# A new order, engine assignment and buffer choice for the same work: pooled attention with a gated convolution feed-forward, one Trainium2 core

## The chip, the core and the metric

The kernel runs on one core of one Trainium2 chip. A core has the matrix engine (PE, whose weight loads are shown apart as PEld), the vector engine (DVE), the activation engine (ACT), the general engine (POOL) and a queue engine that issues transfers (SP). Each runs its own instructions strictly in the order in which the program lists them, and waits on semaphores for the others. The metric is device time in microseconds (us) of one execution; the median of three runs is 651.73 us, from 650.28 to 654.78.

## What is computed

Four batches, eight heads, 1152 keys, head size 64. Queries are averaged in pairs, so 576 queries per head. The attention output, 512 features wide, goes through a feed-forward layer with a three-tap convolution in its gate.

```python
q_pool = q.reshape(B, H, S // 2, 2, D).mean(axis=3)
scores = np.matmul(q_pool, k.transpose(0, 1, 3, 2)) / np.sqrt(D)
attn = softmax(scores);  x = attn @ v            # (4, 576, 512) over all heads
h = np.maximum(x @ w_in, 0.0)                    # (4, 576, 1024)
gate = sigmoid(conv3(h, conv_w))                 # three taps along the sequence
out = (h * gate) @ w_out                         # (4, 576, 512)
```

## The kernel before

The program builds a list of 2470 tasks, each with an engine, what it must come after and the buffers that it uses. `Plan.order` (line 62) does not search at run time: it reads three tables. `SWAPPED` names the tasks that run on their other permitted engine, `SLOTS` gives the buffer of each ring that a task takes, and `ORDER` lists the tasks in the order in which they are written out. That fixes the queue of every engine. The numbers given to `add` as costs are not used by `order`, so they leave no mark in the program.

Two heads make a pair; there are 16 pairs, and each has five blocks of 128 queries (the fifth holds 64 of both heads). A block of one head goes through this chain:

- `scores` (L436, PE) multiplies queries and keys into a PSUM tile `s`, of which there are two. `top` (L448, DVE) finds the row maximum, `expo` (L453, ACT) takes the exponential and the row sum into `p`. The `s` tile is free again when `expo` is done. There are 144 of each.
- `total` (L466 on ACT or L470 on DVE) and `inverse` (L476, DVE) make the reciprocal of the sum.
- For most heads `high` (L500 on ACT or L495 on POOL) writes the normalised row in half precision into `hl`, `low` (L503, DVE) writes the remainder, and a transposing transfer (L516, SP) brings both to `pt`. For seven heads `norm` (L534 ACT, L538 POOL or DVE) keeps full precision, PE transposes (L552) into a PSUM tile `a`, of which there are two as well, and ACT copies it out (L557).
- `values` (L582, L588, PE) multiplies by the values; L598 (ACT), L604 or L606 (ACT or POOL) and L611 (DVE) split the result `x` in two halves.

Per batch, `feed` runs over groups of tokens and eight slices of 128 hidden features: `mm` (L671, PE), `relu` (L677, ACT), `tap0` (L684 on ACT or L688 on POOL), two more taps (L695, DVE), `tanh` (L701, ACT), `gate` (L705, DVE). `second` (L873, L879, L885, PE) multiplies by `w_out`, and L899 (ACT) copies out. Queries arrive by a transfer and are first added in pairs by `sum_q` (L289, POOL or DVE), then scaled by ACT (L292, L296). The early part of the kernel also takes the weights apart (L962 to L999).

Of the kernel before, what the change touches and what calls it, by code (L numbers as in the profile page):

```python
# [99 lines left out]
jNeldwkgdxdyj6kuj4khkOdzbFkvbGkidAkPkqdDbhkRehj7emkrkGj5kwbHkxkSkyksbsdtkTbIkBkzkCkHkDkEdEbJk6kjkQkAbKk9kUkFkV  # L100
bLk7kWk3kkk4kZklenbtk0buk5k8bvkmkolabweolokpbMbxknlbeCkXlpbyk1k2lrdKd3dJbQbCbRkKlcbSdLldlsllbTlqbUlmkYlebVltbz
b5lffvlGlnkLbDlubAlJlveFlHlDlhdMlglKlwlidOb6ljdPlkb7lzlLlElxlylYb8lFlIdQb9dRlBcalMdScbmjlZdTeHlNdUl0mklOdXlCdY
mmlAl1cclVlTl2mnl3lPlUlQlRcdeJmbdNmllWbWeGbBmol6eId4l4mBd5lSmpd6l5mEmqmCmrbXmcl7lXmymFmwl8l9mad7mxbYmumDmzd8eW
mTbZmGmAd9b0eamsb1mHmvmImUmJnbmtb2ebmVb3mMecmOb4efmNmWmPnckImdcemQedmKmXmfepkMmLjdmRmYeendmZkJejm0mSegm8eYkNne
m9mgcfmhnOm1nfnaeqcgm2ngmem6chjeerntcinhm3nicjm7nPnqm4e0nGeZjhnuckm5njnrnvclnsjinknQnwcmnRnxminHnBnIn6cwnlnSny
eBe1nmnonnnJnTn7DanpnUnVDCnzDbnWDXnZnADDcxesnXDoDYDEcyDcDFn8n0DdooczDeDpDGn9cADHDqopDZn2n1DfnEn3nFD0n4cBDJn5D1
cCDIDrD2nCoaDKoqDhDLDsobcDorD3cEocnDoGodoscnDioeohfdnKnYofDtDjDkotDMDlDuDmouDnovoHowoknLozcoomoJoxnMonoloicpoI
oKffDQojoLoEcqogoYnNcrDRoMDgDSD4csoFoNoZoOfheEctoyfiDvcuD5oPoReupmcvDwo0evDxoUcFewexD6oAeyoVpjo1D7ezD8oBo2eAoW
oSpko6eDoXfPoToCo3pbDyetpnoQplo4oDD9cGDzo5poEao9cHpEcIpcDNppDAcJfgpBpqcKpafwpucLo7pCprpzo8pApvpxpwcMpyEbpFcNpD
pGDTpTcOpsfceVDOpWpHEcpUpteKEdpfeLpIpXpJpMeMEecPpKpVcQpYEffyqbpZDBp0DUp1pNp4qcqtpgpOp2Egp5Eip6quqdpLcRp7EjcSp8  # L110
p9EkeOqeePqvcTeQEleRpRf6qfqap3cUpPqOeSqgqwqxqBeTqRqhqiqPqmpQpSfzcVqpDVeUqnqqqoqrqSqjeXqGqQeNqkqyEmqsqlqzqTq2fA
cWfBDWEhqUqAq5qVDPqWq3qZEwfNqHqXe3ERExq0qYq4EKq6EyEnEzq7q1rgEAEoESq8rjq9rhrdrae4ELe5fQrkqCETqEqFriEpe6rbEMEUrc
rlrxENe7reEBruqDqKECEOrfe8EPrmrve9rnryrorrEqrprwrsrqrzrIfbrAsdqLrBErrJrFrCrtEYfSseEssfEDrDrZEQrKrErGEEr2rLr0EF
EZrMr3rHrNrOr4E0EVr1rPEGsgfar5rQEWr6rRsar7shr8EtsiE1EHr9sbEIEusjfRsrEJskEvE2EXscsosuE4ssE5rVsvstfeslspsmswsFrS
# [1076 lines left out]
```

## Time and profile before

| | |
|---|---|
| median of three runs | 651.73 us (650.28 to 654.78) |
| the profiled execution | 651.88 us, of which the span of the trace is 650.1 us |
| PE busy | 585.3 us, 90% of the span |
| DVE busy | 580.9 us, 89% |
| ACT busy | 514.1 us, 79% |
| POOL busy | 163.9 us, 25% |

An engine's busy time is the time in which one of its instructions was running. Idle time is put down to whatever ended it. Two engines are near 90%, so the question for any stretch of the kernel is which of the two has the fewer gaps there, and what ends these gaps.

### The profile page before, as it was taken

The page shows a single profiled execution, that of the slowest core. Times are in us where ns is not written, and L with a number is a line of the kernel's source. Part 1 is how long each engine was busy: PE and PEld are TensorE (multiplying, and loading weights), DVE is VectorE, ACT ScalarE, POOL GpSimd, SP SyncE. Part 2 cuts the span into 40 slices and gives each one's busy share as a digit, 9 for nine tenths or more (in the row PEclk, how much of TensorE's full clock was granted, in tenths as well). Part 3 has the DMA queues.
Part 4 walks back from the last instruction along what each step waited for, and adds up shares of the span by engine and source line. Part 5 has one row for each costly group of instructions (what it writes and reads, how often), then busy time and mean ns, then how long its engine had stood idle before and what let it go on. Part 6 is the DMA issues. An engine that isn't in the chain of part 4 may idle for free. (4 is left out here: it accounts for less than half of the span.)

```text
span 650.1 us, 11849 instructions
## 1 busy us (share of the span) xinstructions
PE 585.3 (90%) x4394; PEld 364.9 (56%) x4394; DVE 580.9 (89%) x930; ACT 514.1 (79%) x959; POOL 163.9 (25%) x174
## 2 busy tenths in 40 slices
PE   3578887889998899999999899999999879999997
...
GB/s 302 176 188 202 187 155 148 160 160 125 164 142 218 130 184 171 180 211 173 218 138 219 175 207 182 169 211 182 199 163 200 199 152 129 200 111 151 91 34 40
DMA packets 276569, 109.61 MB, mean 169 GB/s; under 512 B 264864, under 2 KB 265376, under 8 KB 276512
## 3 DMA queue, kind: packets, MB, share of 16 engines
...
q8 instruction: 34, 0.56, 0.4%
...
## 5 line engine op out<-in xcount | busy, mean ns | idle before, releaser
L453 ACT ACTIVATE p<-s,sm 128x1152 f32<-128x1152 f32 x144 | 175.1, 1217 | 65.6 <-DVE sm L448 33.1
L436 PE MATMUL s<-kt,qt 64*128 64x512 f32 (+3 forms) x704 | 190.1, 484 | 34.0 <-ACT p L453 24.8
L448 DVE TENSOR_REDUCE sm<-s 128x1 f32<-128x1152 f32 x144 | 193.0, 1347 | 7.4 <-PE s L436 6.7
L503 DVE SCALAR_TENSOR_TENSOR hl<-p,sm,hl 128x1152 f16<-128x1152 f32 (+1 forms) x116 | 172.5, 1493 | 13.8 <-POOL hl L495 9.1
L436 PEld LDWEIGHTS s<-kt,qt 64*128 64x128 f32 (+1 forms) x704 | 92.2, 178 | 137.6 <-issue 79.6
L436 PE MATMUL s<-kt,qd 64*128 64x512 f32 x256 | 149.2, 665 | 0.0
L495 POOL TENSOR_SCALAR hl<-p,sm 128x1152 f16<-128x1152 f32 (+1 forms) x54 | 73.2, 1356 | 208.0 <-DVE sm L476 135.8
L582 PE MATMUL a<-pt,v 128*64 128x256 f16 (+2 forms) x1566 | 119.5, 271 | 0.4 <-ACT h L677 0.4
L671 PE MATMUL a<-x,wi 128*128 128x257 f16 (+3 forms) x864 | 104.8, 274 | 3.1 <-ACT pt L557 1.0
L582 PEld LDWEIGHTS <-v 128*64 128x64 f16 x1566 | 92.1, 110 | 10.3 <-issue 3.9
L671 PEld LDWEIGHTS <-wi 128*128 128x128 f16 x864 | 77.1, 98 | 29.5 <-issue 9.9
L879 PE MATMUL a<-wo,g 128*128 128x512 f32 x192 | 89.3, 606 | 0.7 <-DVE vs L334 0.7
L500 ACT ACTIVATE hl<-p,sm 128x1152 f16<-128x1152 f32 (+1 forms) x62 | 77.3, 1250 | 7.0 <-DVE sm L476 6.6
L695 DVE SCALAR_TENSOR_TENSOR g<-h,cw,g 128x255 f32<-128x255 f32 (+3 forms) x144 | 67.5, 488 | 4.7 <-ACT g L684 3.0
L552 PE MATMUL a<-ident,p 128*128 128x128 f32 (+1 forms) x315 | 49.8, 284 | 18.3 <-ACT pt L557 9.4
L588 PE MATMUL a<-pt,v 128*64 128x256 f32 (+1 forms) x252 | 64.3, 409 | 0.3 <-ACT pt L557 0.3
L879 PEld LDWEIGHTS a<-wo,g 128*128 128x128 f32 x192 | 34.6, 192 | 37.2 <-issue 34.9
L552 PEld LDWEIGHTS a<-ident,p 128*128 128x128 f32 (+1 forms) x315 | 33.3, 146 | 32.9 <-ACT pt L557 11.6
L557 ACT ACTIVATE pt<-a 128x384 f32<-128x384 f32 (+2 forms) x98 | 44.1, 473 | 8.1 <-PE a L552 7.8
L677 ACT ACTIVATE h<-a,bs 128x257 f32<-128x257 f32 (+3 forms) x72 | 33.8, 470 | 18.7 <-PE a L671 14.0
L688 POOL TENSOR_SCALAR g<-h,cw 128x255 f32<-128x255 f32 (+3 forms) x27 | 20.0, 743 | 102.2 <-ACT h L677 84.2
L538 POOL TENSOR_SCALAR p<-p,sm 128x1152 f32<-128x1152 f32 (+1 forms) x16 | 23.5, 1466 | 77.6 <-DVE sm L476 63.4
...
## 6 DMA issues: line engine op xcount, KB each, us to landing
...
```

The costliest lines, as they stand in the source:

```text
L436: nc.tensor.matmul(out=w, lhsT=f, rhs=kk, start=True, stop=True)
L448: nc.vector.tensor_reduce(out=sm[:, e:e + 1], in_=runs(st[e]), axis=AX.XY, op=ALU.max, negate=True)
L453: nc.scalar.activation(out=p.tile().rearrange("p (a n) -> p a n", a=2), in_=runs(st[e]), func=AF.Exp, bias=sm[:, e:e + 1], scale=1.0, accu ...
L495: eng.tensor_scalar(out=hl[rows, 0], in0=ps_[e][rows], scalar1=sm[rows, 6 + e:7 + e], scalar2=1.0, op0=ALU.mult, op1=ALU.mult,)
L500: nc.scalar.activation(out=hl[rows, 0], in_=ps_[e][rows], func=AF.Copy, scale=sm[rows, 6 + e:7 + e])
L503: nc.vector.scalar_tensor_tensor(out=hl[rows, 1], in0=ps_[e][rows], scalar=sm[rows, 6 + e:7 + e], in1=hl[rows, 0], op0=ALU.mult, op1=ALU.s ...
L552: nc.tensor.transpose(w[:, (i - a1) * nq:(i - a1 + 1) * nq], ps_[e][rows, i * P:(i + 1) * P], ident[rows, rows])
L582: nc.tensor.matmul(out=to, lhsT=o.v[:, e, c, vc:vc + D], rhs=o.pt[y, e][:, hl * NC + c, 0:n], start=(c == 0 and j == 0), stop=(c == NC - 1 ...
L588: nc.tensor.matmul(out=to, lhsT=o.v[:, e, c].bitcast(F32), rhs=p32.rearrange("p (a n) -> p a n", a=NC)[:, c, 0:n], start=(c == 0), stop=(c ...
L671: nc.tensor.matmul(out=w[:, 0:n], lhsT=wi[:, a, j, f * P:(f + 1) * P], rhs=x.x[:, c, s0:s0 + n], start=(i == 0 and j == 0), stop=(i == 2 a ...
L695: nc.vector.scalar_tensor_tensor(out=c, in0=h[:, t:t + tok], scalar=cw[:, f, t:t + 1], in1=c, op0=ALU.mult, op1=ALU.add)
L879: nc.tensor.matmul(out=w.tile(), lhsT=g[f // 4][:, f % 4, c:c + P], rhs=wo[:, f, :], start=(f == 0), stop=(f == FC - 1),)
```

## The change

`ORDER` and `SLOTS` are new throughout and `SWAPPED` names 170 tasks where it named 193. 155 tasks have another engine. Counted by line the engines change as follows; all else stays on its engine.

| task | before | after |
|---|---|---|
| `tap0` | 45 ACT, 27 POOL | 61 ACT, 11 POOL |
| `high` of the scores | 62 ACT, 54 POOL | 65 ACT, 51 POOL |
| `high` of x | 22 ACT, 14 POOL | 24 ACT, 12 POOL |
| `norm` | 16 POOL, 12 DVE, 7 ACT | 18 POOL, 10 DVE, 7 ACT |
| `total` | 48 ACT, 32 DVE | 45 ACT, 35 DVE |
| `sum_q` | 9 POOL, 7 DVE | 8 POOL, 8 DVE |
| last join of the weights (L999) | 6 POOL, 11 DVE | 4 POOL, 13 DVE |
| first half of v (L368, L373) | 10 ACT, 6 POOL | 9 ACT, 7 POOL |
| first half of w_out (L809, L813) | 4 ACT | 3 ACT, 1 POOL |

Two cost numbers in `add` are new as well. The diff, with one line of each table:

```diff
 ORDER = """
-cYaacXc1c2aucZc0abbNc3acadc4aehOafagahavaihRajhPaEdhawdihQhSh6axhTayazhUbOhVhWh9aAh7aFh3aBhXaGh8iaaChZioh4c5aD
...
+cYaacXc1c3bNauabcZc2acadc4aehOafagahbOaihRajhPavaEc0awhQdihSdBdhh6bPhTaxayhUhVazhWh9aAh7h3aBh1c6h4h8hZiaaCaFio
...
 SWAPPED = """
-aiaMaWa6bqbwbybVcdcmcvcEcWc1dfdldFezeTeYfyfJf4gkgBgJgUhbhhhJhUiciuiwiDiMi1i3i6jhjpjrjyjJjQjZkhkqkwkykBkMlelllu
...
+aiaMaWa6bqbwbybMbVb4cdcmcvcEcWc1dfdldFedeTe9fyfJf9gBgJgUg0hbhhhJhUiliuiwiDiMi3i6jpjJjQkjkqkykBkMkUlclelllMl1mp
...
         o.qts = [tq] + [
-            add("ACT", act(K1, 0.03), lambda e=e: turn_q(e), after=[t], uses=[o.qin] + ([o.qd] if e else []),
+            add("ACT", act(K1, 0.16), lambda e=e: turn_q(e), after=[t], uses=[o.qin] + ([o.qd] if e else []),
...
-            t = add("ACT", act(tok, 0.14), tap0, alt=("POOL", 0.28 + tok / 1400.0, True), after=[t] + cw_ready, uses=[h] + ([] if first else [g]),
+            t = add("ACT", act(tok, 0.14), tap0, alt=("POOL", 0.36 + tok / 1500.0, True), after=[t] + cw_ready, uses=[h] + ([] if first else [g]),
```

Three places show what this does to the queues. The first is DVE in batch 2, where the profiled execution stood at 355 to 363 us. `p` is the exponential of a block, `hl` its normalised halves, `sm` its sums. Before:

```order
L376 SCALAR_TENSOR_TENSOR v<-vin,vs,v 128x9x64
L538 TENSOR_SCALAR p<-p,sm 128x1152
L476 RECIPROCAL sm<-sm 128x2
L503 SCALAR_TENSOR_TENSOR hl<-p,sm,hl 128x1152
L448 TENSOR_REDUCE sm<-s 128x1
```

The same place on DVE in the change:

```order
L470 SCALAR_TENSOR_TENSOR sm<-sm,small 128x2
L476 RECIPROCAL sm<-sm 128x2
L705 SCALAR_TENSOR_TENSOR g<-g,h 128x255
L326 TENSOR_SCALAR vs<-vs 128x1
L503 SCALAR_TENSOR_TENSOR hl<-p,sm,hl 128x1152
L334 TENSOR_REDUCE vs<-a 128x1
```

Between the reciprocal and the L503 that needs the row normalised with it there was nothing, and now there are two short instructions. The `high` between them moved from POOL (L495, followed there by a `sum_q`, L289) to ACT (L500), and that `sum_q` moved to DVE, further on.

The second place is DVE one batch earlier, at 281 to 288 us of the profiled execution, with the names of before. Before:

```order
L476 RECIPROCAL sm<-sm 128x2
L503 SCALAR_TENSOR_TENSOR hl<-p,sm,hl 128x1152 x2
L470 SCALAR_TENSOR_TENSOR sm<-sm,small 128x2
L476 RECIPROCAL sm<-sm 128x2
L448 TENSOR_REDUCE sm<-s 128x1
L503 SCALAR_TENSOR_TENSOR hl<-p,sm,hl 128x1152
```

In the change:

```order
L448 TENSOR_REDUCE sm<-s 128x1
L503 SCALAR_TENSOR_TENSOR hl<-p,sm,hl 128x1152
L448 TENSOR_REDUCE sm<-s 128x1
L476 RECIPROCAL sm<-sm 128x2
L503 SCALAR_TENSOR_TENSOR hl<-p,sm,hl 128x1152
L448 TENSOR_REDUCE sm<-s 128x1
```

Here it is the other way round: a maximum (L448) stood between the last reciprocal and the last L503, and now it stands ahead of the reciprocal, with `high` still on POOL.

The third place is a `tap0` of batch 1 that POOL ran at 248 us, between two `high`. POOL before:

```order
L289 TENSOR_TENSOR qin<-qin 128x640
L368 TENSOR_SCALAR v<-vin,vs 128x18x64
L495 TENSOR_SCALAR hl<-p,sm 128x1152
L688 TENSOR_SCALAR g<-h,cw 128x321
L495 TENSOR_SCALAR hl<-p,sm 128x1152
```

ACT in the change, where the same `tap0` now stands (`h` is the hidden slice, `g` its gate, `cw` the taps):

```order
L598 ACTIVATE xf<-a,vs 128x256
L453 ACTIVATE p,sm<-s,sm 128x1152
L677 ACTIVATE h<-a,bs 128x323
L684 ACTIVATE g<-h,cw 128x321
L677 ACTIVATE h<-a,bs 128x323
L453 ACTIVATE p,sm<-s,sm 128x1152
```

The `tap0` moved from a queue that is idle three quarters of the time to one between two exponentials, right behind the `relu` (L677) that makes its input.

## Rows read from the trace of the kernel before

**Rows 1.** Stretches: us, busy us (instructions) of PE, PEld, DVE, ACT, POOL; clock, DMA, GB/s.
```profile
0.00:50.00 50.00, 27.64 (x109) 15.44 (x109) 41.26 (x66) 39.64 (x74) 10.70 (x15) 0.83 0.81 225
50.00:250.00 200.00, 177.73 (x1306) 115.99 (x1308) 191.85 (x307) 176.25 (x340) 65.75 (x64) 0.98 0.72 163
250.00:500.00 250.00, 241.88 (x1757) 146.76 (x1752) 230.66 (x342) 201.44 (x348) 58.49 (x62) 1.00 0.96 187
500.00:550.00 50.00, 43.22 (x348) 27.29 (x346) 47.80 (x73) 34.95 (x59) 11.22 (x12) 0.97 0.89 161
550.00:650.10 100.10, 94.80 (x882) 59.47 (x880) 69.34 (x146) 61.77 (x141) 17.73 (x22) 1.00 0.53 108
```

**Rows 2.** Chain that ended last, its end: start us, us, what.
```profile
622.45 0.87 issue
623.32 0.70 ACT o L899
...
633.31 9.06 PE a L873 x42
```

**Rows 3.** Groups by shape: line engine op, count | busy us, mean ns | idle before.
```profile
L448 DVE TENSOR_REDUCE sm<-s 128x1 f32<-128x1152 f32 x144 | 193.0, 1347 | 7.4 <-PE s L436 6.7
...
L453 ACT ACTIVATE p<-s,sm 128x1152 f32<-128x1152 f32 x144 | 175.1, 1217 | 65.6 <-DVE sm L448 33.1 <-DVE hl L503 16.5 <-POOL qin L289 2.8
...
L503 DVE SCALAR_TENSOR_TENSOR hl<-p,sm,hl 128x1152 f16<-128x1152 f32 x109 | 161.7, 1490 | 13.7 <-POOL hl L495 9.1 <-ACT hl L500 4.0
...
L500 ACT ACTIVATE hl<-p,sm 128x1152 f16<-128x1152 f32 x60 | 74.8, 1250 | 7.0 <-DVE sm L476 6.6
...
L557 ACT ACTIVATE pt<-a 128x384 f32<-128x384 f32 x84 | 38.6, 483 | 6.1 <-PE a L552 5.8
...
L684 ACT ACTIVATE g<-h,cw 128x255 f32<-128x255 f32 x20 | 10.0, 504 | 0.1
...
L684 ACT ACTIVATE g<-h,cw 128x321 f32<-128x321 f32 x15 | 8.4, 560 | 0.2
...
L538 DVE TENSOR_SCALAR p<-p,sm 128x1152 f32<-128x1152 f32 x7 | 6.7, 952 | 0.0
...
L289 DVE TENSOR_TENSOR qin<-qin 128x640 f32<-128x640 f32 x7 | 5.7, 814 | 4.2 <-DMA qin<-in_q_dram 4.2
...
L999 DVE TENSOR_TENSOR wo<-o,wo 128x512 f32<-128x512 f32 x6 | 4.1, 681 | 0.0
```

**Rows 4.** Line L503, the remainder on DVE: duration ns min/median/max.
```profile
L503 DVE SCALAR_TENSOR_TENSOR hl<-p,sm,hl x116: 1397/1410/2730, 19.7 to 600.0; 128x1152 f16<-128x1152 f32 x109, 64x1152 f16<-64x1152 f32 x7
```

**Rows 5.** Timeline at 357 to 363 us, DVE, then POOL: start us, us, instruction, [idle before].
```profile
357.71 0.17 DVE L476 RECIPROCAL sm<-sm 128x2 f32<-128x2 f32 x1 [0.22 <-ACT sm L466]
359.23 2.69 DVE L503 SCALAR_TENSOR_TENSOR hl<-p,sm,hl 128x1152 f16<-128x1152 f32 x1 [1.35 <-POOL hl L495]
...
357.97 1.23 POOL L495 TENSOR_SCALAR hl<-p,sm 128x1152 f16<-128x1152 f32 x1 [4.78 <-DVE sm L476]
359.16 1.54 POOL L289 TENSOR_TENSOR qin<-qin 128x640 f32<-128x640 f32 x1
```

**Rows 6.** Waits over the whole span: us in total, times, longest us.
```profile
ACT p L453 <- DVE sm L448: 33.1, 33, 3.4
...
PE s L436 <- ACT p L453: 24.8, 30, 2.4
...
DVE hl L503 <- POOL hl L495: 9.1, 9, 1.5
...
DVE sm L448 <- PE s L436: 6.7, 14, 1.0
...
DVE hl L503 <- ACT hl L500: 4.0, 6, 1.3
```

**Rows 7.** Timeline of the start, ACT, then PE.
```profile
7.81 1.28 ACT L296 ACTIVATE qd<-qin 64x512 f32<-64x512 f32 x2
...
8.97 1.19 PE L436 MATMUL s<-kt,qt 64*128 64x512 f32 x1 [8.97 <-DMA kt<-in_k_dram]
```

More of the change, by code (lines that the diff above doesn't have):

```diff
@@ L100 @@
[L100 to L114, printed above, removed]
@@ new lines @@
+h2aGc5ibdlaHaDiricaIdmakidaJdnhXipiedoilaKisdCh5h0iqifimhYalaLihiGc7amaMitanaoaNiJapaOdFaqiuardGiviHiiasigijdH
+c8iKiDatdaiIaYdbiEaPiYiwiLiFaQdcaRikddaSiMixdIiNaTaZdeiOiZizdWiyiniViBjja0a1i0iWiCaUa2iTiXdfjkjmiAiUaViPjli1iR
+a3dkjndZiQjEa4i2joa5c9i6iSjBdgd0a6jpd1i9aWi7jajCi3a7bijbaXjqi8i4a8jyjDi5jzd2djjTjFjrjAbjjcbkdpjGjujUjwa9jWjHei
+bljvdEbajxjIbmjJjsjXjQjfjVdJbnjRdqbobbjYbcbdjtjZj0bpj8kbbqdrj9kebebrjOdselkcjgbEjPjSdujKdvkdj1dwjMkfjLktdxjNbf
+kgdybgj4kuj6j5bFdzj2kOkvbGbHdAkhbIj7dDkRkwkikPemkakqbhkGj3bJdtkxkrenkjdVkBekkQkSkybskzkCkHkDkEbtkTk6buksbvkUkF
@@ new lines @@
+kkkVk7k3kWkok9kpk4eokAkmbKkllabwk8k1k5knbxlbkZlobQk2eCbRlcdKlrldbSk0lpllkXlekKbylsbAkYlmbTltbUbCbVbzb5lqljdYlG
+fvbDlndLlJkLlulvbLlkdMlwlHlDdOlhdPeFlilKlxb6lzlylAb7lflElBlLb8lIlFlYdQb9dRcalMmjlCdSlNlZlglOcbeHmkdTlRl0lTcclS
+mmcdlUlVdUbWlPbBdXl1mbeGehlQl2mllWl3mnl6bXl4dNd3mBmobMbYl5mpmEd4mqmCmymcd5lXl7mFmrl9l8mamDd6mzmsd8mtmTbZmGmAd9
+b0mweab1mHmumImUb2nbmJmvmxebmVb3epmKefmQmOeImWncmdkMkImPb4mLmMkJjhcemfecjdeWmXedmNjimYkNeemZjem0mRcfm8cgnemSm1
+mgm9m4mhndm6nfeYejm7ntnangchmem2cinOm3nhcjm5ninunqcknGe0egnPd7njeqnvnre1clnwnQnknxcmnRmiercwnBnsnHn6nIesnynSnl
@@ new lines @@
+nmeZnonJnnnznpDanTn7nADXcxDbcynUDcfdDCnVczDYnZnWcAn2DdDDcBDEn0nXooDZn3n1DFDon8nYD0opcCn4Dpn9cDn5oqDGeED1nCoaff
+nED2orDqnFobcEDhDecnDrnDeBocD3odDsoeDQosohDioGofetDjDtDfnKDHDkcoDgDlotcpcqDuDmcrouDRovoHowDScsoxctoknLoJolDToy
+oIozomoKoionoYnMojcuoLDnogDvcvoMfhoNoZoODJDwoRoPcFeupmf6DxDKDyo0DIoEevDzoSnNoFpjoTDUo1ewfgexeyoWfiezpkoUoXDLoV
+oCeAoAoDcGeDpboQplcHcIo2cJo3pno6oBfwcKpoDMo9o4pBcLpccMpapEDApCppcNo7D4pqo8pucOpDo5pFprpvD5pTpweJpseKpxeLpUptEb
+pGDBD6DNpWcPpHD7pypID8eVEcpzcQEdpXpJpfpMpKpVeMfypApLpYcRcSpZp0cTp1qbp4pgp2p5D9pNp6qcpOp3p7cUeOqtp8EeqdePpPqupR
@@ new lines @@
+DVpQqepSeQcVqvp9qfEiDOqaEfqgeReSqRcWeTqhqiDWqmDPqOeUqjqPEjeXqpfzqnqqqkqoqrEkqGfAElqlqwEgEmfBqxEhEnqSqyqQeNEofN
+qTqzq2qUqsqVq5qAqZqWq3EpqHqXEwq0q4qYEqq6fQrgErExq7ERq1EyrhqBe3rjEse2q8ESq9EzfcrardqErke4qFETqCe5reriEKEtrlrurb
+rfqDrxEUrvqKrmrce6EVEarne7roryrrrwrprsrzrIrqELEArZEWe8rArJEBqLEYrtrBEXrKr0rCrFEZrDrLEMe9rMECrEEDrGfSr1r2fbfaEE
+E0rNr3EFrHfTrOr4sdEGr5rPsgr6ENr7serRrQEusar8sfEOEHE1r9shfREIsbsisrE2EvscsuEJsjEPskssslsorVsvfUfesmswspstsnsIrS
+EQsFsxsyE4sCE5E6sGsqsDsHE7szsJf7sEsTfksAE8sKsUsBsLsMsVE9sNfjsOtaFaE3sQtdtbflfmtcfnFcsRf9FdfogaftfppdteFefqphsS
@@ new lines @@
+qItffstosWqJgbtgfrtrrWsXthfusYtptisPs2rTsZrXqMtjtqs0FfrUs1tss3tls4tCtks5ttperYFuqNtuFgtvtDtzFIFvtAtFgcFwgoFJFx
+FWtEtmFKFBtGtntwt4FLFXtHtxs6fxFMFytIpitJt5tNgqt6tQtOs7FztTFNtRtPFYtKGhgrFCs8FAFPFOGiFZtUFDfMfDtBFiFEFQFRFFs9tS
+fEFjFSt7tyF0FGt8tLGjt9FkFTgsFHGktMtVulfFfGuauotWGlumGaFbucfHuntXuptYFlfPFUfIGbtZfJF3FVuqfKuDfLurF4uGt1fOuEudgt
+ust2ubGmF5GcuHutFmt3uFGouuF1uwuIuYgHt0F2F6GpGduVfVuJGnuKueuOuBuWuzuvuCuLuAuxuZGJuyuXuMuRgGvdFhuSgnGeu0F7uTveuU
+uPgJvvvfuQvgGfu1fWu2u3GKFovhgKgLuhu4gMgYvwvivjvkGgvlvQfXu6u5uiFpvmF8vofZFqf0uNvxvRFrvyf1vzGQvDFsvAGqu9vBGRvavb
@@ new lines @@
+u7f2g0vTu8vSGrf3vrvUf4vcvsvCGLvtvpGsfChCfYv4vVf5F9f8GSvWv7v5vnvqvuvIvXv8v1vYGtv2vZv9GvGuvJv0GTgeGMGUvGv6GNwwGw
+v3wawbwiwcwxGxGCvHwdwfgXFtGVHbwjwyFnwgGDwlGOGEwkvEwmvFwKGywhwnGFgfGGwowzGPwpggwqwLvMweg1wtwAHcGHwuwrwMghwNGzwB
+w1GWwsgiGIHdwOgjG4wPgkw2GAHewvwCw4gmG5M6wQGXvNG6HfglHiGYG7gpGZwRG8HgG0HjwDw5wEwHw6wFHkwSG9wIw3wGxfw7w8Hhxiw9xg
+wTwJG1xhxaG2gvxjxcHlxbguHaxkxdxtHmG3wUxlGBxexwxmxuHpxnHogdgwHqg2gxxxxvHrxoxqgygzgAHsgEgBxrxyxHxpgCvKwVxKg3xIwX
+gDxJxzvLxsxAxLxBxExCychfxFxMxDHtwWxNufxOgFydxSujxVvOxGHuxTxPx4xWyevPxXughhyqx5x6hjx7yfxQhkHOwYyrxRIgHPygHQInIh
@@ new lines @@
+    "11032113002110221310211320100031303210100112102321100112031020023020101041310221001100213101022302032111012031"
+    "01002110101100210021113122012110130020312000213141102011230203112310110212231010003131231030000110020021101001"
+    "01220020110101203002132140302003011303021111011020131001132100200001110010003112111100311120300011101312200020"
+    "31001011110031030112123001311000020203032100301010011100000301031212102101103113002100211200131110211001130200"
+    "1131012321010110001100"
@@ L159 @@
+mymHmQmZm1nqnwnynBnMnUnZocouoMoOoRo1ppprpupJpMp4qjqmqwqyqUqWq8rdrrrCrLrNr5sjsosLsNs4titutKtYufujurutuwuLu1u3vo
+vyvDvOvWvYwowqwtwCwHwNwVwZw7xcxExYx0ynyPy0zbzlzzzLzZz4AdAoAwAEAMA0A5BgBjBsBDBFB1B6ChCkCyCMCSC8DLEyFDGqGxGLGSJc
+KhKvL8MUNe
 """
```

63 lines of the change are left out of this document (20 added, 43 removed).

## The prediction

> **What bounds the kernel now.** I read the busy times in five stretches first [rows 1]. The reader should look for the engine with the least idle time in each, because that one sets the pace. From 0 to 50 us the kernel fills: DVE is idle for 8.7 us, PE for 22.4. From 50 to 250 us DVE sets the pace, idle for 200 - 191.85 = 8.2 us, while PE is idle for 22.3 and ACT for 23.8. From 250 to 500 us PE does, idle for 8.1 us (DVE 19.3). From 500 to 550 us it is DVE again, idle for 2.2 us, and from 550 us on PE, idle for 5.3 us. PE's figure is the softer one, since its matmuls are pipelined. Added up, the engine that sets the pace is idle for 8.7 + 8.2 + 8.1 + 2.2 + 5.3 = 32.5 us; without the filling it is 23.8 us. That is all that a new order can win without taking work off PE and DVE. The chain that ended last shows at its end what little is left there: PE's products in a row, broken by a wait of 0.87 us and a copy of 0.70 us [rows 2].
>
> I then asked what ends the gaps. DVE waits 13.1 us in 15 places for a `high` before its L503, and 6.7 us in 14 places for scores; PE waits 24.8 us for exponentials, ACT 33.1 us for maxima [rows 6]. ACT and POOL are never the engine with the least idle time [rows 1].
>
> **The change, part by part.** The sum is made against the profiled execution: 651.9 us, of which 1.8 us lie around the span of 650.1. That is 0.2 us over the median of the runs.
>
> *Load.* No arithmetic is added, so PE's load is unchanged. DVE gets two joins at 0.68 us, one `sum_q` at 0.81 and three sums that I put at 0.15, a little under the 0.17 of a reciprocal of the same size [rows 5], and loses two `norm` at 0.95: 1.36 + 0.81 + 0.46 - 1.90 = **+0.7 us**, and I take it as on the path, since DVE sets the pace for 250 us. ACT gets 16 `tap0`, 11 of them of some 255 columns at 0.50 us, 3 of 321 at 0.56 and 2 short ones that I put at 0.3 (below both rows), with three `high` at 1.25 and two more halves of x, which I put at the 0.50 of the shorter `tap0`. It loses three sums, at DVE's 0.15, and one piece of v and one of w_out, for which I take 0.8 and 1.1, between the `tap0` and the `high` of twice the length. Together 5.5 + 1.7 + 0.6 + 3.8 + 1.0 - 0.5 - 1.9 = 10.2 us [rows 3]. ACT is idle for 650.1 - 514.1 = 136 us, 23.8 of it in the stretch from 50 to 250 us, so I cost it at nothing. If that cover fails it costs up to the whole 10.2 us; that is rival C. POOL loses 20 of its 168 instructions and is idle for three quarters of the span: nothing. The two new cost numbers leave no mark in the program.
>
> *Waits for `high`.* The reciprocal and the L503 that follows are both on DVE, with a `high` on another engine between them. What DVE does between the two is the cover. I went through both orders, gave each instruction its mean time from the trace, and took it as short wherever the cover is less than the other engine's instruction and 0.1 us. I did the same for the other waits of this kind on DVE (an exponential before a sum, a `tanh` before a gate, and so on). Before, 33 places are short by 14.1 us together; in the change 32 by 14.4. They are other places. At 359 us the cover was nothing, and DVE waited 1.35 us [rows 5]; with the gate now in between it would be short by 0.8. At 284 us a maximum of 1.35 us [rows 3] covered the `high`, and now nothing does, so 1.4 us is late there that was not. Stalls of over 1 us are six before and six after. The sum gets **+0.3 us**. Its ends are none of the 13.1 us that DVE now waits for `high` [rows 6], and twice that.
>
> *DVE and POOL in each other's way.* The L503 at 359.23 us took 2.69 us, where the median of all 116 is 1.41 [rows 4, 5]. It started when its `high` on POOL was done, and at that moment POOL began the `sum_q` behind it, which ran until 360.70; 360.70 - 359.23 = 1.47 us, and the 1.22 us left are a little less than a normal L503. The 109 L503 of the main shape together are 161.7 - 109 x 1.41 = 8.0 us over that median [rows 3]. The 20 instructions fewer on POOL are 12% of its count, so I take **-1.0 us**; the ends are 0, if other POOL instructions hit instead, and -8.0, if all such meetings go.
>
> The Trainium skill, page "SBUF — State Buffer", section "Who interferes with whom", has a rule for this: a DVE instruction with two inputs in SBUF and a GpSimd instruction that reads SBUF share a port pair, the first to start holds it throughout, and the other blocks entirely. The trace agrees: 2.69 us against 1.41. By that rule it is not the number of POOL instructions that counts but which of them stands ready behind a `high` whose L503 is waiting. I count five such places before and five in the change, so by the rule this term would be 0 and the sum 1.0 us higher.
>
> *PSUM tiles.* A block of scores can start when the exponential of the block two before has freed its `s` tile: a maximum of 1.35 us and an exponential of 1.22, with the steps around them 2.7 us [rows 3]. I added PE's instructions between one block and the next in the same tile. It is less than 2.7 us at 12 places before, short by 8.8 us together, and at 9 in the change, short by 6.5. For the `a` tiles I set 0.6 us, one copy of 0.48 [rows 3] and the steps around it: 48 places short by 11.4 us, and in the change 37 by 6.7. Most of that lies before 250 us, where PE's waits cost only what reaches DVE, that is some of the 6.7 us of waiting for scores [rows 6]. Scaled by 6.5 / 8.8 it is 1.7 us less. Between 250 and 500 us, where PE sets the pace, `s` gets 1.2 us worse and `a` 2.1 us better. Together **-2.6 us**; the ends are 0 and the whole 7.0 us.
>
> *Start and end.* At the start the two L296 and the L292 change places around the L962. The first score waits for its keys until 8.97 us, and the L296 end at 9.1 anyway [rows 7]; nothing. The last products, from 633 us on, stand in the same order [rows 2]: nothing.
>
> Sum: 651.9 + 0.7 + 0.3 - 1.0 - 2.6 = **649.3 us**.
>
> **The rivals.**
>
> *A, the forecast: waits change places and the sum of them stays.* For it: 33 short places against 32, loads within 1 us. Within 1% of 651.7, that is 645.2 to 658.2, about what a measurement of this kernel can tell from no change. Also here belongs the case that the new order lies in the slack altogether and nothing moves (652).
>
> *B, faster: the new order closes gaps that my local count doesn't see.* The pace-setter's 23.8 us are many short gaps, and only some of them are waits that a count of cover finds. PE's tiles do get more cover in the change. If four tenths of the 23.8 us go, the time is 651.9 - 9.5 = 642.4 us. Against it: the same number of stalls of over 1 us.
>
> *C, slower: ACT's queue.* ACT runs in order, and the 16 `tap0` now stand between exponentials. Where an exponential is already awaited, each delays it by 0.5 us, and with it the next scores, maxima and L503. Up to the 72nd exponential ACT has 6 us more ahead of it. It decides from the point at which ACT's idle time in 50 to 250 us, 23.8 us, is no longer where the exponentials need it. If all 10.2 us land on the path, with the +0.7 and +0.3 above and none of the gains, it is 663; with most of it, 660. Against it: ACT itself waits 33.1 us for maxima [rows 6], so it often is early.
>
> *D, slower: DVE blocked by POOL.* If behind each of the six stalls of over 1 us in the change a ready POOL instruction starts first, as at 359 us, that is 6 x 1.3 = 7.8 us; 649.3 + 1.0 + 7.8 = 658. Against it: before has the same pattern, and its cost is in the 651.9 already.
>
> **How the numbers follow.** A 0.51, B 0.31, C 0.11, D 0.07. The likeliest is A, so 649.3 us, with 645 to 654 as its own range. For 8 in 10 the range reaches from 639 us, at which over half of the 23.8 us would be gone, to 658.5, which takes in D: what stays out is the far end of B (0.1) and most of C (0.1). Faster by over 1% is B with 0.02 of A's lower end: 0.33. Slower by over 1% is C, half of D and 0.02 of A's upper end, rounded up: 0.17. The rest, 0.50, is within 1%.
>
> **What would show it.** In the profile of the change the table of stretches should have DVE idle for about 8 us and PE for about 8 us where each sets the pace; under 4 us in both is B. DVE's waits for `high` should again be about 13 us, with one of over 1 us at the second place shown above, and PE's wait for exponentials below 24.8 us. ACT's busy time should be about 524 us and POOL's about 149. If the group of L503 falls well under 1.49 us in the mean, the POOL term was too small; if DVE's waits for exponentials and sums grow by several us and ACT's wait for maxima shrinks, it is C. The prediction is wrong if short gaps, which a count by place can't see, add up to more than the four terms do.

## The result, and the profile after

| | before | change |
|---|---|---|
| first measurement, median | 651.38 us | 645.82 us (641.79 to 646.64) |
| ratio, 95% interval | | 0.9897 (0.9860 to 0.9933) |
| second measurement, median | 651.95 us | 646.02 us (644.50 to 646.61) |
| ratio, 95% interval | | 0.9882 (0.9848 to 0.9917) |

The change is faster by 5.6 to 5.9 us, on the border of the 1% that the forecast called no change. It lies in the range (639.0 to 658.5), 3.3 to 3.5 us under the forecast of 649.3, about halfway from there to the 642.4 us of rival B.

Two profiles of the change were taken. The first is the quickest of its twelve executions, 641.79 us; the second, from the repeat e9 below, is typical at 645.7 us. The busy times of the first, from its page, and of the second:

```profile
PE 579.7 (91%) x4394; PEld 362.0 (57%) x4394; DVE 577.5 (90%) x934; ACT 523.2 (82%) x975; POOL 155.2 (24%) x154
```

```profile
PE 582.3 (90%) x4394; PEld 363.3 (56%) x4394; DVE 580.0 (90%) x934; ACT 523.9 (81%) x975; POOL 153.8 (24%) x154
```

The stretches of the first profile, to lay beside [rows 1] (same columns), and those of the second:

```profile
50.00:250.00 200.00, 178.76 (x1322) 115.66 (x1321) 194.39 (x311) 182.15 (x351) 65.61 (x59) 1.00 0.77 166
250.00:500.00 250.00, 242.81 (x1817) 149.53 (x1816) 233.60 (x357) 209.37 (x358) 49.60 (x52) 1.00 0.99 192
500.00:550.00 50.00, 45.31 (x296) 26.04 (x294) 44.38 (x63) 30.88 (x53) 15.07 (x14) 1.00 0.91 175
```

```profile
50.00:250.00 200.00, 177.49 (x1311) 115.35 (x1308) 192.61 (x306) 178.79 (x344) 62.86 (x57) 0.98 0.73 162
250.00:500.00 250.00, 242.78 (x1793) 148.60 (x1793) 234.24 (x356) 209.48 (x358) 51.23 (x53) 1.00 1.00 193
500.00:550.00 50.00, 45.30 (x318) 26.50 (x313) 45.62 (x67) 33.31 (x57) 14.20 (x14) 1.00 0.89 174
```

DVE idles 5.6 and 7.4 us from 50 to 250 us (before 8.2), PE 7.2 us from 250 to 500 us in both (before 8.1). By the marks of the forecast that is case A; under 4 us in both would have been B. The waits of the second profile, to lay beside [rows 6]:

```profile
ACT p L453 <- DVE sm L448: 24.2, 26, 3.0
...
PE s L436 <- ACT p L453: 21.0, 28, 1.7
...
DVE sm L448 <- PE s L436: 8.4, 14, 1.3
...
DVE hl L503 <- POOL hl L495: 6.7, 7, 1.5
...
DVE hl L503 <- ACT hl L500: 5.5, 9, 1.2
```

The groups by shape of the second profile, to lay beside [rows 3]:

```profile
L453 ACT ACTIVATE p<-s,sm 128x1152 f32<-128x1152 f32 x144 | 175.4, 1218 | 49.3 <-DVE sm L448 24.2 <-DVE hl L503 17.5 <-PE a L552 2.6
...
L503 DVE SCALAR_TENSOR_TENSOR hl<-p,sm,hl 128x1152 f16<-128x1152 f32 x109 | 157.7, 1455 | 12.4 <-POOL hl L495 6.7 <-ACT hl L500 4.9
...
L684 ACT ACTIVATE g<-h,cw 128x255 f32<-128x255 f32 x28 | 13.7, 501 | 0.3
```

ACT waits 24.2 us for maxima after 33.1, with more of its own to do (28 of the short `tap0` after 20), and L503 takes 4.0 us less. DVE's waits for `high` are 12.2 us after 13.1. The one forecast at the second place is there, with the reciprocal directly ahead of it (timeline of DVE, first profile):

```profile
277.19 0.15 DVE L476 RECIPROCAL sm<-sm 128x2 f32<-128x2 f32 x1
278.71 1.42 DVE L503 SCALAR_TENSOR_TENSOR hl<-p,sm,hl 128x1152 f16<-128x1152 f32 x1 [1.36 <-POOL hl L495]
```

To see where time goes I follow the starts of the maxima (L448): the 19th, 64th, 91st, 127th and 136th of 144, counted in the trace, and the end of the issue of the last output transfer.

| start, us | before | change, 1st | change, 2nd | 2nd less before |
|---|---|---|---|---|
| 19th maximum | 77.6 | 76.9 | 80.4 | +2.7 |
| 64th | 252.5 | 246.6 | 250.3 | -2.3 |
| 91st | 361.8 | 353.0 | 356.6 | -5.2 |
| 127th | 510.8 | 502.4 | 506.1 | -4.7 |
| 136th | 545.2 | 533.8 | 537.5 | -7.7 |
| last output issued | 647.6 | 637.5 | 641.4 | -6.2 |

The two profiles of the change differ by 3.5 us at the 19th maximum and by 3.6 to 4.0 us at all later rows. So nearly all of the difference arises ahead of the 19th maximum; where, is read under e9 below.

### The profile page after: what moved, and what is told of

Same layout as the page of the kernel before. It is cut to its first block, busy times and chain, and to the rows that moved or that the text cites. A ratio compares the mean times of both kernels' runs of the same rounds, so it can differ in the third digit from the quotient of the medians.

```text
span 639.9 us, 11873 instructions
## 1 busy us (share of the span) xinstructions
PE 579.7 (91%) x4394; PEld 362.0 (57%) x4394; DVE 577.5 (90%) x934; ACT 523.2 (82%) x975; POOL 155.2 (24%) x154
## 5 line engine op out<-in xcount | busy, mean ns | idle before, releaser
L436 PE MATMUL s<-kt,qt 64*128 64x512 f32 (+3 forms) x704 | 187.4, 476 | 30.2 <-ACT p L453 21.5
L448 DVE TENSOR_REDUCE sm<-s 128x1 f32<-128x1152 f32 x144 | 193.2, 1347 | 8.4 <-PE s L436 7.8
L503 DVE SCALAR_TENSOR_TENSOR hl<-p,sm,hl 128x1152 f16<-128x1152 f32 (+1 forms) x116 | 165.5, 1434 | 13.1 <-POOL hl L495 6.7
L436 PE MATMUL s<-kt,qd 64*128 64x512 f32 x256 | 146.5, 654 | 0.0
L495 POOL TENSOR_SCALAR hl<-p,sm 128x1152 f16<-128x1152 f32 (+1 forms) x51 | 72.8, 1428 | 248.3 <-DVE sm L476 167.8
L500 ACT ACTIVATE hl<-p,sm 128x1152 f16<-128x1152 f32 (+1 forms) x65 | 81.2, 1251 | 19.4 <-DVE sm L476 9.8
L695 DVE SCALAR_TENSOR_TENSOR g<-h,cw,g 128x255 f32<-128x255 f32 (+3 forms) x144 | 70.6, 506 | 6.4 <-ACT g L684 4.8
L538 POOL TENSOR_SCALAR p<-p,sm 128x1152 f32<-128x1152 f32 (+1 forms) x18 | 25.0, 1387 | 63.4 <-DVE sm L476 54.6
L588 PEld LDWEIGHTS a<-pt,v 128*64 128x64 f32 x252 | 33.4, 137 | 10.8 <-issue 0.7
L436 PEld LDWEIGHTS s<-kt,qd 64*128 64x128 f32 x256 | 39.4, 193 | 0.0
```

What stands on the lines that cost most here:

```text
L436: nc.tensor.matmul(out=w, lhsT=f, rhs=kk, start=True, stop=True)
L448: nc.vector.tensor_reduce(out=sm[:, e:e + 1], in_=runs(st[e]), axis=AX.XY, op=ALU.max, negate=True)
L495: eng.tensor_scalar(out=hl[rows, 0], in0=ps_[e][rows], scalar1=sm[rows, 6 + e:7 + e], scalar2=1.0, op0=ALU.mult, op1=ALU.mult,)
L500: nc.scalar.activation(out=hl[rows, 0], in_=ps_[e][rows], func=AF.Copy, scale=sm[rows, 6 + e:7 + e])
L503: nc.vector.scalar_tensor_tensor(out=hl[rows, 1], in0=ps_[e][rows], scalar=sm[rows, 6 + e:7 + e], in1=hl[rows, 0], op0=ALU.mult, op1=ALU.s ...
L588: nc.tensor.matmul(out=to, lhsT=o.v[:, e, c].bitcast(F32), rhs=p32.rearrange("p (a n) -> p a n", a=NC)[:, c, 0:n], start=(c == 0), stop=(c ...
```

## The experiments

**Parts of the change.** The engines alone (e1: the table `SWAPPED` of the change in the kernel before), and order and buffers alone (e2: `ORDER` and `SLOTS`).

```diff
 SWAPPED = """
-aiaMaWa6bqbwbybVcdcmcvcEcWc1dfdldFezeTeYfyfJf4gkgBgJgUhbhhhJhUiciuiwiDiMi1i3i6jhjpjrjyjJjQjZkhkqkwkykBkMlelllu
...
+aiaMaWa6bqbwbybMbVb4cdcmcvcEcWc1dfdldFedeTe9fyfJf9gBgJgUg0hbhhhJhUiliuiwiDiMi3i6jpjJjQkjkqkykBkMkUlclelllMl1mp
...
```

> The order and the buffers of before, with the engine assignment of the change (155 tasks on another engine, POOL 20 instructions fewer, ACT some 10 us more work). Theory 1, the gain of 5.6 us (651.4 to 645.8) comes from POOL and DVE meeting less often: it shows here already, 647 to 649 us, and the mean of L503 (1.490 us before, 1.435 in the change) falls below 1.46. Theory 2, the gain is in the order and the assignment only serves it: no gain, 651 to 655 us, since ACT gets tasks at places where the old order did not plan for them, with DVE's waits for ACT above those of before. Theory 3, ACT's load hurts by itself: 656 us or more.

> The order and the buffers of the change, with the engine assignment of before. Theory 1 (POOL and DVE meeting less): the gain is lost, 650 to 653 us, with the mean of L503 back at about 1.48 us. Theory 2 (the order alone brings it): most of the gain stays, 646 to 648 us. If both this and the assignment alone are slower than before, the two only fit each other, and neither has a share of its own.

e1 took 673.93 us, ratio 1.0358 (1.030 to 1.041), and e2 668.20 us, 1.0259 (1.020 to 1.032). In e1, DVE idles 200 - 179.41 = 20.6 us from 50 to 250 us, and waits for `high` on ACT 12.6 us, where it was 4.0 [rows 6]. Its stretch (columns as in [rows 1]), then its row of waits:

```profile
50.00:250.00 200.00, 172.37 (x1229) 112.64 (x1230) 179.41 (x289) 174.19 (x337) 60.80 (x56) 0.95 0.68 158
```

```profile
DVE hl L503 <- ACT hl L500: 12.6, 14, 2.5
```

So the engines don't carry the gain, nor does the order: each costs 18 to 24 us without the other. e1 alone would be theory 3, ACT's load by itself; but e2, without that load, is nearly as slow. So what came true is the last sentence on e2: the two fit each other. The same assignment is dear in one order and not in the other. Its 16 `tap0` on ACT are a part of 155 moves, and e1 doesn't show what they cost by themselves.

**Halves of the change.** e3 has the change's tables up to the 65th block and those of before behind it, e4 the reverse. One line of e3's diff:

```diff
 ORDER = """
-cYaacXc1c2aucZc0abbNc3acadc4aehOafagahavaihRajhPaEdhawdihQhSh6axhTayazhUbOhVhWh9aAh7aFh3aBhXaGh8iaaChZioh4c5aD
...
+cYaacXc1c3bNauabcZc2acadc4aehOafagahbOaihRajhPavaEc0awhQdihSdBdhh6bPhTaxayhUhVazhWh9aAh7h3aBh1c6h4h8hZiaaCaFio
...
```

> Order, assignment and buffers of the change for its first 1060 tasks (up to the 65th of 144 score blocks, about 250 us, where DVE sets the pace), then all the rest as in before. Theory A, the gain comes from the stretch where DVE sets the pace (the 64th maximum starts 5.9 us earlier in the change): 645 to 647 us, and the 64th maximum at 246 to 248 us. Theory B, the second part gives back what the first wins because PE sets the pace there and has its own load: 649 to 651 us, with the lead of 6 us shrinking after 250 us. Theory C, the gain is at the end (the last 18 blocks): 651 us.

> The mirror: order, assignment and buffers of before for its first 1060 tasks (65 score blocks, about 250 us), then all the rest as in the change. Theory A (gain in the stretch where DVE sets the pace): 650 to 652 us, the 64th maximum at 252 to 253 us. Theory C (gain in the later part): 646 to 648 us. If this and the mirror together win more than the change does, the joint of the two tables costs nothing and there is more to win by mixing.

e3: 653.89 us, ratio 1.0033 (1.0001 to 1.0064); e4: 648.94 us, 0.9968 (0.9945 to 0.9991). e3 is outside all three of its expectations. By the medians it has none of the gain, 3.6 us over before, and e4 has 1.3 us of it. What follows is read from one profile of each. In e3 the 64th maximum starts 2.4 us earlier than before; the joint, where two unrelated orders meet, costs 2.7 us between the 64th and the 73rd. In e4 the part behind the joint gains 3.6 us (+1.2 at the 64th maximum, -2.4 at the end). 2.4 + 3.6 is 6.0 us, the gain of the whole. But up to the 64th maximum e4 has the queues of before and is 1.2 us late there, and e6 below 1.5 us, so each of the two shares is good to no more than that, and e4's holds the price of its own joint. That the gain is spread over both halves is the likely reading; it is not shown.

**The price of DVE time.** Ten maxima over a constant, read by nobody, on DVE: in blocks 13 to 58 (e5) or 69 to 123 (e6) of the kernel before. 13.4 us in both.

```diff
+    def idle_dve():
+        nc.vector.tensor_reduce(out=spare, in_=ident[:, None, :].to_broadcast([P, 9, P]), axis=AX.XY, op=ALU.max)
+
+    for _ in range(10):
+        add("DVE", 1.3, idle_dve)
```

> The kernel before with ten idle reductions on DVE of about 1.35 us each, one behind every fifth maximum from the 13th to the 58th, where DVE sets the pace by the table of stretches (50 to 250 us). If that reading holds, nearly all of the 13.5 us lands in the time: 10 to 14 us more than before (650.2), so 660 to 664. If the gaps of 8 us in that stretch, or waits elsewhere, take them up: 5 us or less.

> The same ten reductions on DVE, but behind every sixth maximum from the 69th to the 123rd, where PE sets the pace by the table of stretches (250 to 500 us, DVE idle for 19 us there). If a DVE wait costs only where DVE sets the pace, 0 to 5 us more than before (650.2), so 650 to 655; then the waits for high that the prediction counted all alike should have been counted in the first stretch alone. If PE and DVE are so closely coupled that each wait of either costs everywhere, 9 to 14 us more, as in the mirror.

e5: 662.86 us, ratio 1.0193 (1.013 to 1.025); e6: 664.47 us, 1.0211 (1.016 to 1.026). The medians are 12.3 and 13.9 us above the 650.54 us of before, 92% and 104% of what was added; the intervals reach from 8.6 to 16.5 and from 10.4 to 17.0 us. The profiles give less. In e5 the 64th maximum starts 10.6 us late and nothing is added after it: 79% of 13.4. In e6 the delay grows from 1.5 us at the 64th to 10.7 us at the 127th: 9.2 us, 69%, in the part where I had let PE set the pace and DVE had 19.3 us idle [rows 1]; 1.4 us more come behind the 127th. So the price is 0.7 to 1.0 of what was added, in both stretches.

**The price of ACT time.** Sixteen copies of 0.517 us, 8.3 us, on ACT behind every third exponential of blocks 13 to 58 in the kernel before.

```diff
+    def idle_act():
+        nc.scalar.activation(out=spare, in_=ident[:, None, :].to_broadcast([P, 3, P]), func=AF.Copy)
+
+    for _ in range(16):
+        add("ACT", 0.5, idle_act)
```

> The kernel before with 16 idle copies on ACT of about 0.45 us (7 us in all), one behind every third exponential from the 13th to the 58th. It measures the price of ACT's load, which the prediction set to nothing and its rival C to nearly all. By the forecast 0 to 2 us more than before (650.2); by rival C 5 to 8 us more.

656.23 us, ratio 1.0067 (1.0034 to 1.0099); that is 5.7 us over before by the medians and 2.2 to 6.4 us by the interval, nearer to rival C's 5 to 8 us than to the 0 to 2 us of the forecast. The 64th maximum starts 3.6 us late: 44% of 8.3 us, on an engine that was idle for 23.8 us from 50 to 250 us [rows 1]. Two more steps, of 1.4 and 1.7 us, follow behind the 91st and the 127th maximum, where nothing was added. At both places PE's granted clock is lower than in the kernel before: 0.50 from 369 to 372 us, after a gap of 1.77 us on PE, where before has 1.00; and 0.50 from 537 to 543 us, where before has it for half as long.

**POOL out of DVE's way.** The kernel before with its nine `sum_q` on DVE.

```diff
 SWAPPED = """
-aiaMaWa6bqbwbybVcdcmcvcEcWc1dfdldFezeTeYfyfJf4gkgBgJgUhbhhhJhUiciuiwiDiMi1i3i6jhjpjrjyjJjQjZkhkqkwkykBkMlelllu
...
+aiaMaWa6bqbwbybVcdcmcvcEcWc1dfdldFdZelezeFeTeYfffyfJfQf4f9gkgqgBgJgUg0hbhhhyhJhUiciuiwiDiMi1i3i6jhjpjrjyjJjQjZ
...
```

> The kernel before with the nine sum_q that POOL had moved to DVE, at their places in the order. DVE gets 9 x 0.81 = 7.3 us more work, and loses the time for which a sum_q on POOL blocked it: 5.8 us on L503 in the profile of before, 8.5 us with the other instructions. If blocking is worth what the trace shows, the two nearly cancel: 648 to 652 us, with the mean of L503 at 1.43 to 1.45 us. If a blocked L503 is only shown long and costs nothing on the path: 655 to 658 us.

647.93 us, ratio 0.9945 (0.9917 to 0.9973). The group of L503, which was 161.7 us [rows 3]:

```profile
L503 DVE SCALAR_TENSOR_TENSOR hl<-p,sm,hl 128x1152 f16<-128x1152 f32 x109 | 157.4, 1451 | 13.7 <-POOL hl L495 9.1 <-ACT hl L500 4.0
```

I also added up, over all DVE instructions that meet one of POOL, what each took beyond the median of its shape. That is 18.1 us before and 9.2 us here: DVE got nine instructions and was yet less busy, 578.8 us against 580.9. By the medians this small edit alone brings 2.6 us, nearly half of the change's gain.

**The change once more.**

> The change once more, unaltered, as the measure for the three kernels beside it and for the spread of its profile. Its profiled execution was the quickest of its six (641.8 us; the others 644.3 to 646.6) and had 13.6 us of PE at half clock inside the kernel, where before had 27.2 us. If such windows make the spread, at some 1.4 us for each 3.4 us of them, a second profile near 645 us shows about 20 to 27 us at half clock, the same order of waits, and DVE idle from 50 to 250 us again under 6.5 us. If the quick profile was only luck in DVE's waits, the half-clock total stays near 14 us and DVE's idle time from 50 to 250 us is back at 8 us. Median 645 to 646.5, ratio 0.989 to 0.994.

Nothing is edited. 646.02 us. What parts the two profiles lies between 65 and 79 us. First profile, timeline of DVE, POOL and PE:

```profile
66.39 0.16 DVE L470 SCALAR_TENSOR_TENSOR sm<-sm,small 128x2 f32<-128x2 f32 x1
...
67.37 0.69 DVE L999 TENSOR_TENSOR wo<-g,wo 128x512 f32<-128x512 f32 x1
...
68.12 1.42 DVE L503 SCALAR_TENSOR_TENSOR hl<-p,sm,hl 128x1152 f16<-128x1152 f32 x1
...
68.24 2.69 POOL L289 TENSOR_TENSOR qin<-qin 128x640 f32<-128x640 f32 x1 [5.14 <-DMA qin<-in_q_dram]
...
70.40 0.32 PE L331 MATMUL a<-ident,vs 128*128 128x128 f32 x1 [0.65 <-ACT xf L598]
```

Second profile, the same instructions, with the `norm` of POOL:

```profile
65.81 1.74 POOL L289 TENSOR_TENSOR qin<-qin 128x640 f32<-128x640 f32 x1 [2.96 <-DMA qin<-in_q_dram]
66.17 1.40 DVE L470 SCALAR_TENSOR_TENSOR sm<-sm,small 128x2 f32<-128x2 f32 x1
67.94 1.51 POOL L538 TENSOR_SCALAR p<-p,sm 128x1152 f32<-128x1152 f32 x1 [0.39 <-DVE sm L476]
68.39 1.60 DVE L999 TENSOR_TENSOR wo<-g,wo 128x512 f32<-128x512 f32 x1
71.59 0.33 PE L331 MATMUL a<-ident,vs 128*128 128x128 f32 x1 [2.09 <-DVE vs L326]
```

The stretches behind them in the second profile (columns as in [rows 1]):

```profile
72.00:76.00 4.00, 3.41 (x16) 1.39 (x17) 3.26 (x9) 3.20 (x6) 0.83 (x1) 0.50 0.22 42
76.00:80.00 4.00, 4.00 (x23) 2.49 (x17) 2.60 (x6) 1.82 (x5) 1.15 (x2) 0.68 0.00 0
```

The first profile had this from 71 to 79 us:

```profile
71.00:79.00 8.00, 6.91 (x53) 4.16 (x53) 7.47 (x20) 7.38 (x16) 4.71 (x6) 1.00 0.30 67
```

In the second profile the queries landed 2.4 us earlier. So `sum_q` started on POOL ahead of the L470, a two-element sum, which then took 1.40 us in place of 0.16; the `norm` behind it made the L999 take 1.60 in place of 0.69. DVE was 2 us late, PE stood idle for 2.09 us, and after that its clock was granted at 0.50, the lower level (1.2 GHz), until about 79 us; in the first profile it stays at 1.00 there. Ahead of it the 10th maximum starts at 43.3 and 43.4 us; behind it the stages agree within 0.4 us. So the 3.5 us arise here, some 2 us by DVE's delay and the rest while PE runs at the lower clock. The early transfer began it in this execution, but e10 shows the same stretch without a `sum_q` on POOL. Of the expectation one mark came true, 20.5 us at half clock where 13.6 are named for the first profile, with this stretch as the 6.8 us more. The other did not: DVE idles 7.4 us from 50 to 250 us, where under 6.5 was expected. Nor do such stretches alone make the spread of the change's times: an execution of 646.61 us has a mean granted clock of 0.987, next to the 0.988 of the one of 641.79 us.

**The change with its `sum_q` on DVE.** Eight tasks leave POOL.

```diff
-aiaMaWa6bqbwbybMbVb4cdcmcvcEcWc1dfdldFedeTe9fyfJf9gBgJgUg0hbhhhJhUiliuiwiDiMi3i6jpjJjQkjkqkykBkMkUlclelllMl1mp
...
+aiaMaWa6bqbwbybMbVb4cdcmcvcEcWc1dfdldFdZedeleFeTeYe9fffyfJfQf9gqgBgJgUg0hbhhhyhJhUiliuiwiDiMi3i6jpjJjQkjkqkykB
...
```

> The change, with the eight sum_q that its POOL computes put on DVE; order and slots stay. The same edit made the kernel before 3 us quicker (647.9 against 650.5): POOL had blocked DVE for 18.1 us there and then for 9.2 us, while DVE got nine instructions of 0.81 us. Theory 1, it is the blocked time less the added load that counts: in the change the sum_q block DVE for only 4.3 us of 15.3, and DVE gets 8 x 0.81 = 6.5 us, so DVE has 2.2 us more to do and at 0.7 of that the time goes up by 1.5 us (647). Theory 2, moving sum_q off POOL is worth as much here as there: 3 us less (643). Theory 3, the order was fitted to the places of sum_q on POOL, as to every other place: over 5 us slower.

644.20 us (643.08 to 645.13), ratio 0.9856 (0.9822 to 0.9890): 1.8 us under the change on the same chip, and the quickest kernel here. It lies between theory 1, 1.5 us more, and theory 2, 3 us less. The blocked time went from 17.7 (e9) to 12.7 us, a fall of 5.0 us, less than the 6.5 us that DVE got, so theory 1 falls; DVE's busy time is 580.4 us against 580.0, and its idle time shrank from 643.9 - 580.0 = 63.9 us to 61.8. Why the added work went into the idle time here I haven't shown. In DVE's timeline the L470 at 66 us takes 0.16 again; the L999 is still blocked for 0.9 us by the `norm`:

```profile
65.90 0.16 DVE L470 SCALAR_TENSOR_TENSOR sm<-sm,small 128x2 f32<-128x2 f32 x1
...
66.89 1.60 DVE L999 TENSOR_TENSOR wo<-g,wo 128x512 f32<-128x512 f32 x1
```

But PE's clock falls here as well, after gaps of 0.85 and 1.36 us on PE. The row of PE, then the stretch:

```profile
72.19 0.90 PE L552 MATMUL a<-ident,p 128*128 128x128 f32 x3 [1.36 <-DVE vs L334]
```

```profile
71.00:79.00 8.00, 6.51 (x28) 3.54 (x29) 6.09 (x15) 4.68 (x9) 1.99 (x2) 0.57 0.04 7
```

The 19th maximum starts at 79.7 us, 0.6 us ahead of e9 and 2.8 us behind the first profile, with the 0.81 us of this `sum_q` now on DVE at that very place. The four later profiles, e9 to e12, all have an L999 of 1.60 us and a stretch at the lower clock from 72 or 73 us on. So the first profile is the exception, and a `sum_q` on POOL is not needed for most of the loss.

**Waits covered by hand.** In e11, 36 DVE instructions of the change stand earlier in DVE's own order, in 13.3 us of waits. One of them, as rows of DVE's queue (`sum_q` is L289):

```diff
 L476 RECIPROCAL sm<-sm 128x2
-L503 SCALAR_TENSOR_TENSOR hl<-p,sm,hl 128x1152
-L448 TENSOR_REDUCE sm<-s 128x1
...
 L289 TENSOR_TENSOR qin<-qin 128x640
+L503 SCALAR_TENSOR_TENSOR hl<-p,sm,hl 128x1152
+L448 TENSOR_REDUCE sm<-s 128x1
...
```

> The change, with 36 DVE instructions put earlier in DVE's own order, each directly ahead of an instruction that waited 0.3 to 1.7 us in the change's profile, each ready by the start of that wait and no longer than it. Engines, slots and the order on all other engines stay. Together they would fill 13.3 us of DVE's idle time. Theory 1, DVE's idle time costs about 0.7 wherever it lies (as ten added DVE instructions of 1.34 us cost 9.2 to 10.6 us of 13.4): 13.3 x 0.7 = 9.3 us less, 636.5 us. Theory 2, the waiting instruction is on the path and the filling only lets a later instruction finish early, so the wait comes back at a later place: 643 to 647 us, with DVE's idle time as large as before the edit. Theory 3, an instruction put ahead delays an awaited one by up to its own length whenever the run's waits lie elsewhere than in the profile: slower by 2 us and more.

> Both edits together: the eight sum_q on DVE and the 36 DVE instructions put earlier (two of the 36 are sum_q, which then fill the waits at 278 and 351 us). If the waits filled count at 0.7 and the blocked time as in theory 1 of the sum_q run, 646 - 9.3 + 1.5 = 638 us. If neither counts, 643 to 648 us. If the sum is the two single results added to within 1 us, the two edits are independent; if it is worse by over 2 us, DVE has no room for both.

e11: 650.66 us, ratio 0.9969 (0.9938 to 1.0001), 4.6 us slower than the change. Theory 1 is out. Most of the loss lies at the two `sum_q` among the 36: their queries had not landed, where I had taken the issue of the transfer for its end. Timeline of DVE in e11:

```profile
285.07 0.83 DVE L289 TENSOR_TENSOR qin<-qin 128x640 f32<-128x640 f32 x1 [2.51 <-DMA qin<-in_q_dram]
...
359.60 0.83 DVE L289 TENSOR_TENSOR qin<-qin 128x640 f32<-128x640 f32 x1 [3.01 <-DMA qin<-in_q_dram]
```

Waits of 1.36 and 0.93 us became 2.51 and 3.01, and the 64th to 91st maximum took 3.7 us more than in e9; 1.1 us more were lost by the 19th maximum, ahead of any move. The other moves are the cleaner test. Behind the 91st maximum 28 instructions, 9.9 us, fill waits: from there to the 127th e11 takes 149.3 us against 149.5 in e9, and from the 127th to the end 135.3 against 135.3. Covering returned nothing, as theory 2 has it. But it was tried only where little could come back: from the 91st to the 127th maximum PE is idle for 4.8 of 149.5 us in e9, and DVE for 7.8; from there to its last product PE is idle for 6.8 us. Ahead of the 64th maximum, where DVE is idle for less than PE, only two of the moves lie, 0.6 us together. What cover would return there is not shown.

e12, both edits, took 649.69 us, ratio 0.9951 (0.9925 to 0.9978). The single results add to +4.6 - 1.8 = +2.8 us over the change; +3.7 was measured, within 1 us of it.

## Why the prediction was right or wrong

**Right: the range, and most of the marks.** The waits changed places: 13.1 us for `high` became 12.2, with the forecast 1.36 us at the second place; ACT came to 523 and 524 us (forecast 524); PE's wait for exponentials fell to 21.5 and 21.0 us, as [rows 6] with the term on PSUM had it; PE's idle time from 250 to 500 us is 7.2 us. POOL missed its mark, with 155.2 and 153.8 us for about 149. Rivals C and D did not happen. But what gave case A its name did not hold: the sum of the waits did not stay. DVE's idle time in the span fell from 69.2 to 63.9 us in the typical profile and PE's from 64.8 to 61.6. That the result fell into the range is owed in part to its width.

**Load, +0.7 and -1.0 with the POOL term.** Together -0.3 us of DVE time; DVE's busy time fell by 0.9 us in the typical profile and 3.4 in the quick one. The POOL term was put at -1.0 by the count of POOL's instructions, 20 of 168 (the trace has 174). L503's group fell by 4.0 us in the typical profile, from 161.7 us [rows 3]. But other two-input instructions were hit in its place: over all of DVE the blocked time is 18.1 us before, 15.3 in the first profile of the change and 17.7 in the second. By the Trainium skill ("SBUF — State Buffer", section "Who interferes with whom") it is the order of issue that decides who blocks; worked out by that rule, the prediction's term was 0. The second profile agrees, with -0.4 us; the first has -2.8 us, so the two don't decide between 0 and my -1.0. Looking at L503 alone, whose mean fell from 1.490 to 1.455 us, misleads. The row at 66 us shows that even a two-element L470 waits out a `sum_q`.

**ACT at nothing.** The kernel did not get slower, but the reason given was wrong. e7 shows that 8.3 us on ACT cost 3.6 us or more although 23.8 us were idle, and e1 that the change's own assignment costs 23.7 us in another order. So idle time of ACT doesn't make its load free. What the load costs within the change no run shows; that the new order has room for it is my reading.

**Which engine sets the pace: the step that failed.** I gave each stretch one pace-setter and let waits of the other pass. e5 and e6 price DVE time at 0.7 to 1.0 in the two stretches, so DVE is on the path in both, also where PE has less idle time; and ACT, which I had on no path, costs 0.4 and more (e7). e11 doesn't add to this: that filled waits of DVE return nothing where PE is idle for 3% is also what a single pace-setter would give. That PE, DVE and ACT wait for each other in turn within each block is how I read the rows of waits. So a count of cover on DVE alone cannot price a wait, and "four tenths of the pace-setter's idle time" in rival B had nothing to stand on; of that idle time, 4.1 us lie behind PE's last product, where no order wins anything. The mixed waits behind the PSUM term show the same: scores waited less for exponentials (-3.8 us), and DVE waited more for scores (+1.7), where I had scaled that down. Between 250 and 500 us, where I had priced PE's own waits, the term fits: 0.9 us less idle time on PE.

**The size.** The sum was -2.6 us; measured were -5.6 and -5.9. The term for waits on DVE had the wrong sign, +0.3, where its waits for `high` fell by 0.9 us and its idle time by 5.3. Two of the largest falls on DVE are not in the prediction's rows: the L334, a short maximum that waits for the product L331, from 3.7 us to 0.3 or less in both profiles, and the gate (L705), which waits for its `tanh` (L701), from 4.9 to 1.9. Their rows before, columns as in [rows 6]:

```profile
DVE vs L334 <- PE a L331: 3.7, 3, 2.2
...
DVE g L705 <- ACT g L701: 4.9, 7, 1.0
```

How much of these waits the time follows is not shown. In the typical profile the span is 6.2 us shorter: PE's idle time fell by 3.2 us, about what the waits were to bring, and its busy time by 3.0, from 585.3 to 582.3 us, where I wrote that PE's load is unchanged. The load is, but not its duration. PE's clock, for which the sum has no term, is a part of it. It is read off the rows of the kernel before, where PE ran at the lower clock after a gap at 529 us (stretches, columns as in [rows 1]):

```profile
529.00:532.00 3.00, 0.58 (x4) 0.39 (x5) 3.00 (x4) 1.51 (x3) 0.00 (x0) 0.97 0.63 121
532.00:535.00 3.00, 3.00 (x8) 1.24 (x6) 2.00 (x3) 1.95 (x3) 1.22 (x1) 0.50 0.96 109
```

e3 and e8, which run the same instructions there, stayed at 1.00 and took 1.4 us less from the 127th to the 136th maximum; the change has no such stretch there. Their rows, e3 first:

```profile
526.00:538.00 12.00, 9.51 (x30) 4.36 (x29) 11.90 (x16) 6.53 (x12) 3.57 (x3) 1.00 0.88 142
526.00:538.00 12.00, 9.52 (x51) 4.97 (x52) 11.90 (x23) 6.38 (x12) 1.45 (x2) 1.00 0.91 152
```

In all, PE was at the lower clock for 27.3 us of the span before and for 20.5 us in the typical profile. At 1.4 us for the 3.4 us of the stretch at 532 us, the 6.8 us less are worth 2.8 us, an estimate that would cover nearly all of the 3.0. The clock is not the whole gain: the two executions of the change with a mean granted clock of 0.976 took 646.4 and 646.6 us, and the 13 of the kernel before at the same clock 648.6 to 656.2. That the rest is many short waits and no single cause fits e3 and e4, as far as they can tell; which of the waits it is stays open.
